# Linear attention and a SiLU MLP on one core: another token layout, two load queues, and transposes by DMA

## The chip, the cores and the metric

The kernel runs on one core of a Trainium2 chip. The metric is the device time of one execution in microseconds (us); a profile's span is the time from the first to the last instruction of one execution. Engines are named as in the profile: PE (TensorE), DVE (VectorE), ACT (ScalarE), POOL (GpSimd) and SP (SyncE); PEld is PE's weight load.

## The reference

```python
# q, k, v: (8, 8, 576, 64) float32: batch, heads, tokens, head size
def phi(x):
    return np.where(x > 0, x, np.exp(x) - 1.0) + 1.0
q_p, k_p = (phi(q), phi(k))
kv = np.einsum('bhsd,bhse->bhde', k_p, v)
z = np.sum(k_p, axis=2)
num = np.einsum('bhsd,bhde->bhse', q_p, kv)
den = np.einsum('bhsd,bhd->bhs', q_p, z)[..., None] + 1e-06
x = (num / den)            # then (batch * tokens, heads * 64) = (4608, 512)
h = x @ w_in               # w_in (512, 2048)
g = h * (1.0 / (1.0 + np.exp(-beta * h)))
out = g @ w_out            # w_out (2048, 512), out (4608, 512) float32
```

## The kernel before

The MLP runs nine times: once for each of the eight batches with its first 512 tokens, and once for the tail, the 64 last tokens of all batches together (`xT_tail`). Each run has an H phase (`h_phase`, L266: 16 groups of four products of 512 columns, and a SiLU on ACT for each group, `g`, L275) and a Y phase (`y_phase`, L291: four output tiles `y_ps` of 16 products each, a copy `y_sb` on DVE, a store by SP). So there are 18 phases of 64 products. The factor 1/beta of the SiLU form is folded into `w_out` by `w_out_scale` (L325, DVE).

Attention of a batch (`elu`, L166, and `attention`, L181) is split into steps which the phases call between their groups (`step(fill)`); nothing reorders them, so each engine takes its instructions in the order in which the code writes them. Attention 0 stands ahead of H0. Attention 1 starts inside Y0 and ends ahead of H1; attention 2, and phi of batch 3, stand in Y1; from batch 3 on attention n stands in H of batch n-1, and phi of batch n in Y of batch n-2.

Tokens of a batch lie as four per partition for the first 512 (`NJ = 4`, tiles of 128 partitions) and a fifth tile of 64 rows. phi is an exponential on ACT (L152), a maximum with 0 (L153), a minimum with 1 (L155) and an addition (L156) on DVE, each over 2560 elements per partition. `kvp` (L191) sums 4 x 5 products of 128 rows and 130 columns (64 of v and a column of ones, for two heads); DVE multiplies them with a mask that leaves the two heads' blocks (`kv_bd`). The numerator needs q with the head size on partitions, and H needs x so: both are transposed by PE against an identity (`qtp` L209, `xtp` L241, four products a token tile) into PSUM and copied by DVE (`q_pT` L213, `xT` L249). A numerator `nps` (L220, four products) gives the numerators and, in each head's 65th column, the denominators; DVE makes `den`, `rden` and `xs` (L228 to L231) of it.

Loads are all issued by POOL (`load_rows`, L62, two DMAs each, cast from fp32 to bf16 on the way), in the order k, v, q of batch 0, four pieces of `w_in`, four of `w_out` (as fp32, into buffers that are free at that time) with q, k, v of batch 1 between them. SP issues the stores and one small load. PSUM has four banks for H and Y (`mmps`), two for one numerator tile (`numps`, one buffer) and two for all else (`miscps`).

## Time and profile before

| | |
|---|---|
| Time, median of 3 runs (lowest to highest) | 358.24 us (358.24 to 358.39) |
| Span of the profiled execution | 355.9 us |
| PE busy | 307.2 us, 86%, 1793 products |
| DVE busy | 167.0 us, 47% |
| ACT busy | 153.2 us, 43% |
| POOL busy | 47.8 us, 13% |
| Bytes moved by DMA | 30.19 MB in 46133 packets |

The profile's page gives no time of the profiled execution other than its span; the median of the runs stands 2.3 us above that span. Busy times of engines overlap, so they don't add up to the span, and PE's busy time contains the latencies of products that overlap their neighbours. A stage table (busy time of each engine between two times), the chain of waits and the timeline show where PE stands still. The column PEclk is the granted clock of PE as a share of 2.4 GHz.

### The profile page before, as it was taken

The numbers are of one execution on the slowest core, as the hardware profiler recorded it, in microseconds if no ns is written. First come the engines' busy times: TensorE is split into PE (matmuls) and PEld (weight loads), VectorE is DVE, ScalarE is ACT, GpSimd is POOL, SyncE is SP. The second block draws the span as 40 slices with busy tenths as digits, with TensorE's granted clock in tenths as the row PEclk, the third lists the DMA queues.
The fourth block names the chain that finished last, engine by engine and source line by source line (L and its number), as shares of the span: only waits on it lengthen the run. The fifth ranks groups of instructions, "written<-read, shape, count | busy, mean of one in ns | idle before, by whom it ended". The sixth has DMA issues, their size and how long they took to land.

```text
span 355.9 us, 4500 instructions
## 1 busy us (share of the span) xinstructions
PE 307.2 (86%) x1793; PEld 153.5 (43%) x1793; DVE 167.0 (47%) x341; ACT 153.2 (43%) x174; POOL 47.8 (13%) x64
## 2 busy tenths in 40 slices
...
GB/s 104 192 275 252 289 175 214 219 52 57 1 168 174 110 1 2 78 207 33 2 66 118 2 0 25 96 1 2 29 90 0 2 71 47 2 59 59 0 61 60
DMA packets 46133, 30.19 MB, mean 85 GB/s; under 512 B 13840, under 2 KB 40480, under 8 KB 46112
## 3 DMA queue, kind: packets, MB, share of 16 engines
q0 software_dynamic: 40832, 20.45, 41.0%
...
HBM read 36.71 MB, written 9.44 MB: 130 GB/s over the span
## 4 chain that ended last, share of the span: by engine, by line
PE 65%; DVE 20%; issue 5%; DMA 4%; ACT 3%; POOL 1%; ACTq 0%; DVEq 0%; POOLq 0%
PE h_ps L271 30%; PE y_ps L296 25%; DVE xs L231 8%; PE xtp L241 5%; PE nps L220 3%; DMA xqk<-in_q_dram 3%; DVE rden L229 2%; ACT e L152 2%; DVE e L155 2%; DVE den L228 2%; DVE y_sb L303 2%; DMA out_dram<-y_sb 2%; PE kvp L191 1%; DVE qk_p L156 1%; DVE xT L249 1%
## 5 line engine op out<-in xcount | busy, mean ns | idle before, releaser
L275 ACT ACTIVATE g<-h_ps,beta_c 128x512 bf16<-128x512 f32 x144 | 98.5, 687 | 120.6 <-PE h_ps L271 119.9
L271 PE MATMUL h_ps<-xT,w_in 128*128 128x512 bf16 x512 | 128.6, 392 | 0.0
L296 PE MATMUL y_ps<-w_out,g 128*128 128x512 bf16 x576 | 127.3, 379 | 0.0
L296 PEld LDWEIGHTS <-g 128*128 128x128 bf16 x576 | 56.0, 98 | 65.8
L271 PEld LDWEIGHTS <-w_in 128*128 128x128 bf16 x576 | 54.1, 100 | 55.3 <-issue 6.2
L303 DVE COPY y_sb<-y_ps 128x512 f32<-128x512 f32 x36 | 24.6, 687 | 83.7 <-PE y_ps L296 77.6
L152 ACT ACTIVATE e<-xqk 128x2560 bf16<-128x2560 bf16 x16 | 36.7, 2331 | 4.6 <-DMA xqk<-in_q_dram 3.1
L241 PE MATMUL xtp<-identity,xs 128*128 128x128 bf16 (+1 forms) x160 | 17.0, 237 | 20.9 <-DVE xs L231 18.8
L155 DVE TENSOR_SCALAR e<-e 128x2560 bf16<-128x2560 bf16 x16 | 13.4, 835 | 38.0 <-ACT e L152 38.0
L275 ACT ACT_TABLE_LOAD x7 | 9.0, 1283 | 51.1 <-PE h_ps L271 51.1
L231 DVE TENSOR_TENSOR xs<-nps,rden 128x512 bf16<-128x512 f32 (+1 forms) x40 | 27.6, 689 | 1.4
L156 DVE TENSOR_TENSOR qk_p<-r,e 128x2560 bf16<-128x2560 bf16 x16 | 23.9, 1492 | 0.5
L241 PEld LDWEIGHTS <-xs 128*128 128x128 bf16 (+1 forms) x160 | 9.7, 105 | 31.3 <-DVE xs L231 31.3
L209 PE MATMUL qtp<-identity,qk_p 128*128 128x128 bf16 (+1 forms) x160 | 15.8, 227 | 6.8 <-DVE kv_bd L197 5.0
L191 PE MATMUL kvp<-vaug,qk_p 128*128 128x130 bf16 x160 | 13.1, 238 | 8.2 <-DVE qk_p L156 8.2
L209 PEld LDWEIGHTS <-qk_p 128*128 128x128 bf16 (+1 forms) x160 | 11.9, 104 | 16.3 <-issue 7.6
L213 DVE COPY q_pT<-qtp 128x512 bf16<-128x512 bf16 (+1 forms) x40 | 15.7, 395 | 6.6 <-PE qtp L209 6.3
L220 PE MATMUL nps<-kv_bd,q_pT 128*128 128x130 bf16 (+1 forms) x160 | 18.3, 244 | 0.3 <-DVE q_pT L213 0.2
...
L249 DVE COPY xT<-xtp 128x512 bf16<-128x512 bf16 x32 | 13.6, 424 | 9.3 <-PE xtp L241 8.2
L220 PEld LDWEIGHTS <-q_pT 128*128 128x128 bf16 (+1 forms) x160 | 13.2, 112 | 8.8 <-issue 2.7
L191 PEld LDWEIGHTS <-qk_p 128*128 128x128 bf16 x160 | 11.6, 107 | 12.0 <-DVE qk_p L156 8.8
...
## 6 DMA issues: line engine op xcount, KB each, us to landing
out_dram<-y_sb SPq DMA_DIRECT2D x32, 256.0 KB, 2.3
...
```

Of the source, the lines that this page charges most:

```text
L152: nc.scalar.activation(e, x, ACTF.Exp)
L155: nc.vector.tensor_scalar(e, e, 1.0, None, ALU.min)
L156: nc.vector.tensor_add(st[b, "p"][:, a].rearrange("p j (h d) -> p h j d", h=H), r, e)
L191: nc.tensor.matmul(kvp[:, pp, :], qk_p[:, 1, j, p * P : (p + 1) * P], va[:, j, 2 * p : 2 * p + 2, 0 : D + 1], start=(j == 0), stop=(j == N ...
L209: nc.tensor.matmul(tp[:, p, :n], qk_p[:n, 0, t, p * P : (p + 1) * P], identity[:n, :n], is_transpose=True, start=True, stop=True, skip_gro ...
L220: nc.tensor.matmul(nps[:n, p // 2, o : o + 2 * (D + 1)], q_pT[:, p, t * P : t * P + n], kv_bd[:, p, :], start=True, stop=True, skip_group_ ...
L231: nc.vector.tensor_mul(xs[t][:n], nv[:, :, :, 0:D], rden[:n, :, :, None].to_broadcast([n, 2, 4, D]),)
L241: nc.tensor.matmul(tp[:, p, :n], xv[:n, p * P : (p + 1) * P], identity[:n, :n], is_transpose=True, start=True, stop=True, skip_group_check ...
L271: nc.tensor.matmul(hp, w_in_sb[ff // 4][:, kc, (ff % 4) * P : (ff % 4 + 1) * P], x[:, kc, :], start=(kc == 0), stop=(kc == KC - 1),)
L275: nc.scalar.activation(g[:, ff, :], hp, ACTF.Silu, scale=beta_c[:, ff : ff + 1])
L296: nc.tensor.matmul(yp, g[:, ff, t * P : (t + 1) * P], w_out_sb[ff // 4][:, ff % 4, :], start=(ff == 0), stop=(ff == FC - 1),)
L303: nc.vector.tensor_copy(y_sb, yp)
```

## The change

All 576 tokens of a batch lie as nine per partition on 64 partitions (`G = 64`, `J = 9`); heads 0 to 3 take the lower 64 partitions and heads 4 to 7 the upper. There are no unused rows any more, and no memory clears. A token tile of a numerator takes two of the nine (four tiles of 128 columns and one of 64); the ninth tokens of all batches form the tail run. kv products have 64 rows each, 36 a batch, and change between the halves and between two PSUM tiles from one to the next (`kv_products`).

phi is min(exp(x), max(x, 0) + 1): an exponential, one DVE instruction for maximum and addition, and one minimum, each over 1152 elements, twice for k and twice for q. v is loaded as fp32 by SP and cast by POOL (for batch 0 it is cast on the way and copied by DVE). k and q are loaded by POOL with the cast; half the heads of k and q of batch 0 come by SP as fp32. `w_out` comes by SP after the third piece of `w_in`; two of its four pieces are scaled by DVE, two by POOL.

`idle` puts products of a constant tile on PE during the opening, whose results nobody reads. H0 starts with four groups of half the columns. Y0 keeps its four tiles open in four PSUM banks and does three quarters of each of them ahead of attention 1. From batch 3 on, q and x are transposed by DMAs that SP issues (`q_trans_dma`, two a batch, `x_trans_dma`, five a batch) instead of by PE; for batches 0 to 2 PE transposes and ACT (batches 0 and 1) or DVE copies. Each Y tile is stored by two DMAs of 64 partitions, from three buffers instead of two. The last Y tile is done in two pieces, of 320 and of 192 columns.

```diff
-    NJ = 4
-    MAIN = NJ * P
-    TAIL = S - MAIN
-    NT = NJ + 1
-    EA = D + 2
+    G = 64
+    J = S // G
+    NT = 5
+    EA = D + 1
...
+    xk = [consts.tile([P, 4, J, D], BF16, name=f"xk{i}") for i in range(NX)]
+    xq = [consts.tile([P, 4, J, D], BF16, name=f"xq{i}") for i in range(NX)]
+    vf = [consts.tile([P, 4, J, D], F32, name=f"vf{i}") for i in range(2)]
+    vaug = [consts.tile([P, 2, J, 2, 66], BF16, name=f"vaug{i}") for i in range(2)]
...
+    w_out_f = [
+        a.rearrange("p (c m) -> p c m", c=4)
+        for a in (g_f[:, 0:2048], g_f[:, 2048:4096], stage[:, 0:2048], stage[:, 2048:4096])
...
+    k0f = stage[:, 0:1152].rearrange("p (h j d) -> p h j d", h=2, j=J)
+    q0f = stage[:, 1152:2304].rearrange("p (h j d) -> p h j d", h=2, j=J)
...
+    def heads(src, b, hh, h0, n):
+        return src[b, hh * 4 + h0 : hh * 4 + h0 + n].rearrange(
+            "h (g j) d -> g h (j d)", j=J
...
+    def load(eng, dst, src, b, h0=0, n=4):
+        return [
+            eng.dma_start(
+                out=dst[hh * G : (hh + 1) * G].rearrange("p h j d -> p h (j d)"),
+                in_=heads(src, b, hh, h0, n),
+            )
+            for hh in range(2)
+        ]
...
+    nc.vector.memset(warm, 0.5)
+    load(nc.gpsimd, xk[0][:, 0:2], k, 0, 0, 2)
+    load(nc.sync, k0f, k, 0, 2, 2)
+    load(nc.gpsimd, xq[0][:, 0:2], q, 0, 0, 2)
+    load(nc.sync, q0f, q, 0, 2, 2)
+    beta_row = consts.tile([FC, P], F32)
+    nc.sync.dma_start(out=beta_row, in_=moe_beta.rearrange("(c p) -> c p", p=P))
+    load(nc.gpsimd, v0b[:, 0:2], v, 0, 0, 2)
+    load(nc.gpsimd, v0b[:, 2:4], v, 0, 2, 2)
...
+    load(nc.gpsimd, xk[1], k, 1)
+    load(nc.gpsimd, xq[1], q, 1)
+
+    def load_w_out(i, after=None):
+        d = nc.sync.dma_start(out=w_out_f[i], in_=w_out_v[:, i * 4 : (i + 1) * 4, :])
+        if after is not None:
+            tc.add_manual_dep(d.ins, after.ins.name, SYNC, reason="share of the queues")
...
+    def phi_part(b, a, pr, x):
+
+        e = work.tile([P, 2, J, D], BF16, tag="e", name="e", bufs=3)
+        nc.scalar.activation(e, x, ACTF.Exp)
+        st[b, a, pr, "e"] = e
+
+    def phi_relu(b, a, pr, x):
+        r = work.tile([P, 2, J, D], BF16, tag="r", name="r", bufs=3)
+        nc.vector.tensor_scalar(r, x, 0.0, 1.0, ALU.max, ALU.add)
+        st[b, a, pr, "r"] = r
+
+    def phi_tile(b, a):
+        st[b, a] = work.tile([P, 2, J, P], BF16, tag=f"phi{a}", name=f"phi_{a}")
+
+    def phi_min(b, a, pr):
+        nc.vector.tensor_tensor(
+            st[b, a][:, pr].rearrange("p j (h d) -> p j h d", h=2),
+            st[b, a, pr, "e"].rearrange("p h j d -> p j h d"),
+            st[b, a, pr, "r"].rearrange("p h j d -> p j h d"),
+            ALU.min,
...
+    def kv_products(b, prs, ps):
+        for pr in prs:
+            for j in range(J):
+                for hh in range(2):
+                    r = slice(hh * G, (hh + 1) * G)
+                    nc.tensor.matmul(
+                        ps[hh, pr],
+                        st[b, "k"][r, pr, j, :],
+                        vaug[b % 2][r, pr, j, :, 0:EA],
+                        start=(j == 0), stop=(j == J - 1), skip_group_check=True,
+                    )
...
+    def kv_both(b):
+
+        t = [miscps.tile([P, 2, 2 * EA], F32, tag="misc", name="kvp") for _ in range(2)]
+        kv_products(b, (0, 1), {(hh, pr): t[hh][:, pr] for hh in range(2) for pr in range(2)})
+        kv_tile(b)
+        for hh in range(2):
+            nc.vector.tensor_mul(
+                st[b, "kv"][:, hh], t[hh], kvmask.rearrange("p a g e -> p a (g e)")
+            )
...
+    def q_trans_dma(b):
+        st[b, "qTd"] = work.tile([P, 2, 2 * J, G], BF16, tag="qT", name="qTd")
+        for hh in range(2):
+            nc.sync.dma_start_transpose(
+                out=st[b, "qTd"][:, hh],
+                in_=st[b, "q"][hh * G : (hh + 1) * G].rearrange("p a j c -> p (a j c)"),
+            )
...
+    def x_trans_dma(b, t):
+        n = P if t < NT - 1 else G
+        nc.sync.dma_start_transpose(
+            out=x_dst(b, t),
+            in_=st[b, "xs", t][:n].rearrange("p a h d -> p (a h d)"),
+        )
...
+    def rows(b, j):
+        return out[b * S : (b + 1) * S, :].rearrange("(g j) m -> j g m", j=J)[j]
+
+    def y_out(b, t, yp, c0=0, c1=512, eng=None):
+        y_sb = work.tile([P, DM], F32, tag="y_sb", name="y_sb", bufs=3)
+        (eng or nc.vector).tensor_copy(y_sb[:, c0:c1], yp[:, c0:c1])
+        for i in range(2):
+            dst = rows(b, 2 * t + i) if b < B else rows(2 * t + i, J - 1)
+            nc.sync.dma_start(out=dst[:, c0:c1], in_=y_sb[i * G : (i + 1) * G, c0:c1])
...
+    def load_kq(b):
+        if b < B:
+            load(nc.gpsimd, xk[b % NX], k, b)
+            load(nc.gpsimd, xq[b % NX], q, b)
+
+    def load_v(b):
+        if b < B:
+            load(nc.sync, vf[b % 2], v, b)
...
+    idle(10)
...
+    phi_all(0, "k")
+    idle(6)
+    phi_all(0, "q")
+    for t in range(2):
+        q_trans(0, t, nc.vector)
+    kvp0 = {}
+    for pr in range(2):
+        v_copy(nc.vector, 0, pr)
+    kv_tile(0)
+    idle(4)
...
+    numer(0, 0)
+    numer(0, 1)
+    x_trans(0, 0, nc.scalar)
+    numer(0, 2)
+    x_trans(0, 1, nc.scalar)
...
+    for ff in range(4):
+        hps[ff] = mm_tile("h_ps")
+        h_mm(0, xT[0], ff, hps[ff], 0, 256)
+        if ff == 0:
+            numer(0, 3)
...
+    load_w_out(0, w_in_dma[2])
+    load_w_out(1)
+    load_w_out(2)
+    load_v(1)
+    load_w_out(3)
...
+    load_kq(2)
+    w_out_scale(nc.vector, 0)
+    w_out_scale(nc.vector, 1)
...
+    yps = [mm_tile("y_ps") for _ in range(4)]
+    phi_all(1, "k")
+    phi_all(1, "q")
+    for i in range(3):
+        if i == 2:
+            w_out_scale(nc.gpsimd, 2)
+        for t in range(4):
+            y_mm(0, t, i, yps[t])
+    for pr in range(2):
+        v_copy(nc.gpsimd, 1, pr)
+    w_out_scale(nc.gpsimd, 3)
+    load_v(2)
+    for t in range(3):
+        q_trans(1, t, nc.scalar)
+    kv_both(1)
+    for t in range(3, NT):
+        q_trans(1, t, nc.scalar)
+    numer(1, 0)
+    y_mm(0, 0, 3, yps[0])
+    numer(1, 1)
+    x_trans(1, 0, nc.scalar)
+    y_mm(0, 1, 3, yps[1])
...
+    for t in range(4):
+        y_out(0, t, yps[t])
+    x_trans(1, 4, nc.scalar)
...
+            if last and t == 3:
+                for c0, c1 in ((0, 320), (320, 512)):
+                    for i in range(4):
+                        y_mm(b, t, i, yp, c0, c1)
+                    y_out(b, t, yp, c0, c1)
+                break
...
+    at(sy, 11, lambda: numer(2, 2), lambda: phi_all(3, "q"))
...
+    at(sy, 14, lambda: numer(2, 4), lambda: phi_all(3, "k"))
...
-        att = lazy(attention, b + 1) if b + 1 < B else wait(0)
-        h_phase(b, xT[b % 3] if b < B else xT_tail, [att])
-        load_next(b + 3)
-        e = lazy(elu, b + 2) if b + 2 < B else wait(0)
-        y_phase(b, [att, e])
-        drain(att)
-        drain(e)
+        n = b + 1
+        sh, sy = {}, {}
+        if b == 2:
+            at(sh, 0, lambda: q_trans_dma(3), lambda: load_kq(4))
+        if n < B:
+            if n == 3:
+                at(sh, 1, lambda: [v_copy(nc.gpsimd, 3, pr) for pr in range(2)], lambda: load_v(4))
+            at(sh, 3, lambda: kv_both(n))
+            for t in range(NT):
+                at(sh, 5 + 2 * t, lambda t=t: numer(n, t))
+                at(sh, 6 + 2 * t, lambda t=t: x_trans_dma(n, t))
+        if n + 1 < B:
+            m = n + 1
+            at(sy, 0, lambda: phi_all(m, "q"))
+            at(sy, 2, lambda: q_trans_dma(m), lambda: load_kq(m + 1))
+            at(sy, 6, lambda: phi_all(m, "k"), lambda: [v_copy(nc.gpsimd, m, pr) for pr in range(2)])
+            at(sy, 7, lambda: load_v(m + 1))
+        h_phase(b, xT[b % 3] if b < B else xT_tail, sh)
+        y_phase(b, sy, last=(b == B))
```

How instructions stand now, at three places. First DVE in the steady part, from the Y copies of a batch (`y_sb`) to the first numerator of the next H phase; `kvp` and `qtp`, `xtp` are PSUM tiles. Before:

```order
L303 COPY y_sb<-y_ps 128x512 x3
L197 TENSOR_TENSOR kv_bd<-kvp,kvmask 128x260 x2
L213 COPY q_pT<-qtp 128x4x128 x2
L228 TENSOR_SCALAR den<-nps 128x8
L229 RECIPROCAL rden<-den 128x8
L231 TENSOR_TENSOR xs<-nps,rden 128x512
L213 COPY q_pT<-qtp 128x4x128
L249 COPY xT_88<-xtp 128x4x128
```

After:

```order
L141 TENSOR_SCALAR r<-xk_73 128x1152 x2
L148 TENSOR_TENSOR phi_k<-e,r 128x1152 x2
L309 COPY y_sb<-y_ps 128x512 x3
L190 TENSOR_TENSOR kv_bd<-kvp,kvmask 128x260 x2
L242 TENSOR_SCALAR den<-nps 128x8
L243 RECIPROCAL rden<-den 128x8
L245 TENSOR_TENSOR xs<-nps,rden 128x512
```

The copies of transposes are gone from between the numerators, and with them PE's products `qtp` and `xtp`.

Second, SP's queue. Before, this is all of it:

```order
L388 UNCONDITIONAL_BRANCH
L118 DMA beta_row<-in_moe_beta_dram 16x128
L283 DMA out_dram<-y_sb 128x512 x32
L287 DMA out_dram<-y_sb 64x512 x8
L388 UNCONDITIONAL_BRANCH
```

After, one steady batch from the first x transpose in an H phase on (`xs` is read, `xT` and `qTd` are written in SBUF):

```order
L271 DMA_TRANSPOSE xT_91<-xs 128x4x128 x4
L271 DMA_TRANSPOSE xT_tail<-xs 128x4x64
L217 DMA_TRANSPOSE qTd<-phi_q 128x18x64 x2
L312 DMA out_dram<-y_sb 64x512 x4
L82 DMA vf_78<-in_v_dram 64x4x576 x2
```

SP now issues the transposes and the loads of v in one queue with the stores, and the first stores of a Y phase stand behind the q transposes.

Third, DVE inside Y1, where attention 2 and phi of batch 3 stand. Before:

```order
L228 TENSOR_SCALAR den<-nps 128x8
L229 RECIPROCAL rden<-den 128x8
L231 TENSOR_TENSOR xs<-nps,rden 128x512
L155 TENSOR_SCALAR e<-e 128x2560
L156 TENSOR_TENSOR qk_p<-r,e 128x8x5x64
L153 TENSOR_SCALAR r<-xqk_72 128x2560
L303 COPY y_sb<-y_ps 128x512
L213 COPY q_pT<-qtp 128x4x128
L249 COPY xT_89<-xtp 128x4x128
```

After:

```order
L309 COPY y_sb<-y_ps 128x512
L242 TENSOR_SCALAR den<-nps 128x8
L243 RECIPROCAL rden<-den 128x8
L245 TENSOR_TENSOR xs<-nps,rden 128x512
L141 TENSOR_SCALAR r<-xq_75 128x1152 x2
L148 TENSOR_TENSOR phi_q<-e,r 128x1152 x2
L267 COPY xT_92<-xtp 128x4x128
L212 COPY qT<-qtp 128x4x64
```

phi of batch 3 still stands between the numerators of batch 2, as two pairs of smaller instructions, and it now takes q first.

## Rows read from the trace of the kernel before

**Rows 1.** Stages of the program, windows view: us, busy time per engine, clock, DMA.
```profile
core 0: us, PE busy (x) PEld busy (x) DVE busy (x) ACT busy (x) POOL busy (x), PEclk, DMA share, GB/s
0.00:32.06 32.06, 10.07 (x81) 7.85 (x82) 20.14 (x49) 7.24 (x4) 17.74 (x28) 1.00 1.18 204
32.06:47.60 15.54, 15.54 (x66) 6.72 (x65) 7.53 (x18) 10.28 (x15) 5.68 (x7) 1.00 1.32 249
47.60:75.17 27.57, 21.58 (x146) 12.08 (x144) 18.88 (x37) 7.84 (x6) 7.55 (x10) 0.84 1.38 189
75.17:91.34 16.17, 16.17 (x67) 6.89 (x65) 1.76 (x3) 10.28 (x15) 1.56 (x2) 0.85 0.33 37
91.34:120.97 29.63, 20.36 (x145) 10.86 (x144) 23.19 (x42) 11.23 (x7) 8.60 (x10) 0.94 1.00 136
120.97:295.05 174.08, 168.11 (x1043) 84.10 (x1042) 89.25 (x183) 84.33 (x97) 6.69 (x8) 0.99 0.20 43
295.05:350.47 55.42, 55.41 (x257) 24.94 (x255) 5.53 (x8) 21.98 (x32) 0.00 (x0) 1.00 0.13 38
76.00:80.00 4.00, 4.00 (x11) 1.52 (x10) 1.03 (x2) 1.37 (x2) 1.56 (x2) 0.51 0.24 24
```

**Rows 2.** Chain of waits, Y3 to Y4: start, us, engine, what.
```profile
178.59 13.81 PE y_ps L296 x64
192.41 0.86 PE h_ps L271 x4
193.27 0.58 PE kvp L191 x10
...
198.59 0.18 DVE den L228
198.79 0.21 DVE rden L229
199.03 0.70 DVE xs L231
...
212.86 1.29 PE y_ps L296 x6
```

**Rows 3.** Timeline, PE and weight loads: start, us, operation, idle before.
```profile
14.77 2.35 PE L191 MATMUL kvp<-vaug,qk_p 128*128 128x130 bf16 x20 [7.46 <-DVE qk_p L156]
...
61.42 1.31 PE L191 MATMUL kvp<-vaug,qk_p 128*128 128x130 bf16 x20
...
135.13 0.17 PEld L209 LDWEIGHTS <-qk_p 64*128 64x128 bf16 x4 [0.42 <-issue]
135.14 0.29 PE L209 MATMUL qtp<-identity,qk_p 64*128 64x64 bf16 x4
```

**Rows 4.** Groups by line and form: busy us, mean ns | idle before.
```profile
L303 DVE COPY y_sb<-y_ps 128x512 f32<-128x512 f32 x36 | 24.6, 687 | 83.7 <-PE y_ps L296 77.6 <-DMA out_dram<-y_sb 6.1
...
L152 ACT ACTIVATE e<-xqk 128x2560 bf16<-128x2560 bf16 x16 | 36.7, 2331 | 4.6 <-DMA xqk<-in_q_dram 3.1 <-DVE qk_p L156 1.5
...
L156 DVE TENSOR_TENSOR qk_p<-r,e 128x2560 bf16<-128x2560 bf16 x16 | 23.9, 1492 | 0.5
...
L153 DVE TENSOR_SCALAR r<-xqk 128x2560 bf16<-128x2560 bf16 x16 | 14.0, 878 | 0.0
...
L213 DVE COPY q_pT<-qtp 128x512 bf16<-128x512 bf16 x32 | 13.4, 422 | 6.6 <-PE qtp L209 6.3
```

**Rows 5.** DMA view: GB/s in 40 slices of 10 to 40 us; median us to landing.
```profile
GB/s 171 185 190 195 175 204 209 208 204 210 205 206 203 214 199 205 209 212 344 404 437 393 388 393 388 243 198 198 196 175 198 197 192 282 393 393 388 415 404 421
...
out_dram<-y_sb SPq DMA_DIRECT2D x32, 256.0 KB, 2.3
```

**Rows 6.** Timeline of the opening, three engines.
```profile
7.02 0.29 PE L131 MATMUL bps<-ident,beta_row 16*128 16x16 f32 x1 [7.02 <-POOL ident masks.py:199]
...
14.50 2.34 ACT L152 ACTIVATE e<-xqk 128x2560 bf16<-128x2560 bf16 x1 [3.07 <-DMA xqk<-in_q_dram]
...
17.27 0.91 POOL L63 DMA_DIRECT2D xqk<-in_k_dram  x1 [1.21 <-DMA w_in<-in_moe_w_in_dram]
```

434 lines of the change are left out of this document (201 added, 233 removed).

## The prediction, made before the result was known

> **What bounds the kernel now.** I read the stage table first [rows 1], with the stages cut where the first H or Y product of a batch starts. The eight batches and the tail batch need 18 phases of 64 products of 512 columns; an undisturbed phase takes 13.81 us [rows 2], as four pure phases show together (55.42) [rows 1]. Eighteen of them are 248.6 of the 355.9 us. The other 107 us are the subject: 32.1 before the first product, 13.8 + 15.8 in the two Y phases that carry attention 1 and 2, 4.1 lost in H0 and H1, 36 in the five H phases that carry attention 3 to 7 (174.08 - 10 x 13.81), and 5.4 after the last product. The chain of one steady batch comes next [rows 2]: H4 lasts 20.45 us, from 192.41 to 212.86. Its 80 small products (kvp, qtp, nps, xtp) cost about 0.057 us each (ten kvp: 0.58), 4.5 us together; the remaining 2.1 us are the places where PE stands until DVE has written xs and the x transposes can begin: the chain goes through den, rden and xs there. So TensorE is the bound in the steady part, and what lies between the batches' dependent steps is the bound before 121 us. ACT and DVE have slack in the steady part.
>
> **The steady part (batches 2 to 6).** The change takes q transposes, x transposes and their PSUM copies off PE and DVE (40 of the 80 small products) and gives them to SP as seven DMA transposes per batch. The kv products grow from 20 to 36, since a batch is now nine pieces of 64 rows in two partition halves; numerators stay at 20. For a 64-row product the nearest row is the q tail's transpose, four with 64 columns in 0.29 us [rows 3]: at 64 columns per 0.027 us (2.4 GHz) the four make 0.11 and 0.18 is left for the latency of the last, so they go at the column rate, as 128-row ones do. I therefore take 0.057 for each kv product of 130 columns: 36 x 0.057 = 2.05. Bounds: 1.0 if the two halves run side by side, 4 if every change of half empties the array. The weight loads of that tail wait for the products ahead (0.42 idle), while 128-row ones are loaded ahead; it costs about 0.1, and I add 0.2 for two changes. H becomes 13.81 + 2.05 + 0.2 + 20 x 0.057 = 17.2, with no xs wait, since the consumer of xs is now a DMA. A numerator comes every two groups of products (1.96 us), and den, rden and xs take 0.18 + 0.21 + 0.70 and some hops [rows 2], about 1.5, so the one PSUM tile for numerators is free in time. Y is 13.81 with 0.1 of hops; a pair is 31.1, five are **155.5** instead of 174.1. Bounds 150.5 (kv at 1.0) to 166 (kv at 4, some waits).
>
> In the trace the two-step transposes hide under nothing, so what replaces them must be hidden: the x transposes of batch n are issued in the H phase before and have at least one Y phase (13.8) until H needs them. The q transposes (b from 4) are issued some 5 us into Y and needed 6 groups into H: 15 us later. No row of before has a DMA transpose. The nearest: a 256 KB store takes 2.3 us from issue to landing, over 100 GB/s [rows 5]. Per pair the transposes move 4 x 128 + 64 + 2 x 288 KB, 1.15 MB; over 31.1 us they stay hidden if they do 37 GB/s together. I take them as hidden. Queued behind them on SP: stores of Y and loads of v; SP reaches the first stores of a Y phase only after the q transposes, which wait for phi (about 5.5 us into Y); the first Y tile is ready at 3.5, has three buffers, so nobody waits. If the cover is gone, each us over 31 costs five.
>
> By the Trainium skill, DMA: Bandwidth & Descriptors, section "Latency and other measured facts", a DMA transpose moves 261 GB/s with a non-contiguous middle dimension: an estimate by that page is 1.1 us for 288 KB, well hidden; no run here shows it yet.
>
> **The opening.** Before: q of batch 0 lands shortly before 14.50, when ACT's second exponential begins after a wait of 3.07 us for it [rows 6]; H0 starts at 32.06. In the new order k and q come first, half of each by SP, so ACT is no longer last. DVE is: ident16 now stands behind eight DMA issues of POOL instead of six (0.7 to 0.91 us each [rows 6]), so the beta product goes from 7.02 [rows 6] to about 8.4, and DVE takes beta (1.1) ahead of the first relu: 9.6. Phi in quarters: relu of 1152 elements 0.45 (0.88 for 2560 [rows 4]; 0.65 from fp32), minimum 0.72 (1.49 for 2560), so 2 x (0.45 + 0.65 + 1.44) = 5.1 and hops: phi q at 15, where before its exponential had only begun. Copies of q transposes and v, 1.6, kv 36 products at 0.057, or at 0.107 at the lower clock: 2 to 3.9. (20 kvp took 2.35 us at 14.77, 1.31 at 61.42 [rows 3]: the first at the pace of the lower level, 1.2 GHz, though the clock column shows 1.00 for the opening.) Then two numerators with their x transposes, about 1.65 a piece, and H0 starts its first half-width groups at about 25.5; the other halves wait for the fifth x tile, 29.4. H0 ends 13.81 - 1.73 later (four half-width groups are 1.73): **41.5** (before 47.60). Bounds 40 to 46. Loads don't speed up: one queue reads w_out at 390 to 420 GB/s already [rows 5] (the rows at half of it are loads cast to 2 bytes). First need of w_in is later than its landing (17.3 before [rows 6], about 1.4 later now), w_out waits for the third w_in piece, about 24, and after that 11 MB on both queues take 28 us: the last w_out is there at about 52, and POOL's four scalings (no row has one; 0.5 to 1 us each taken) end at 55. Y0 needs it at 57.
>
> The Trainium skill speaks against this part: DMA: Bandwidth & Descriptors, "Rules for kernel authors", says that transfers spread over several issuing engines, or to disjoint partition halves, share the same engines and gain no bandwidth. The rate of one queue here agrees; by that rule only the order of the loads can gain, which is all that I count.
>
> **Y0 with attention 1.** Three quarters of all four Y0 tiles go first: 10.36 us, under which ACT (table 1.28, four exponentials of 1.05 from 2.33 for 2560 [rows 4]) and DVE make phi. Then q transposes with ACT copies (0.69 taken, as DVE's Y copy of as many elements [rows 4]), 2.5; kv 2.3; masks and the last transposes 1.4; five numerators through one PSUM tile, 0.25 + 1.1 + hops 0.3 each, 8.2, with the last quarters of Y0 beside them; a Y copy that frees the first H bank, 0.7. Sum 10.4 + 15.2 = **25.6** (before 27.57). Bounds 24 to 29. H1 pays 16.17 before: the clock was granted at 0.51, its lower level of 1.2 GHz, through 76 to 80 [rows 1], after a stage with little PE work. With Y quarters in between the stage is fuller; I take **14.4** (13.8 to 16.2).
>
> **Y1 with attention 2 and phi 3.** DVE's list here: phi 2 and 3, 4 x 2.34 = 9.4; five numerators 5.7; q and x copies 4.0 (0.42 each, 0.29 the tails [rows 4]); masks 0.85; four Y copies 2.75: 22.7, and it begins 3.2 after the stage's start (table, first exponential); PE and DVE wait for each other about 1 us more. **27.0** against 29.63 (DVE 23.19 busy there [rows 1]). Bounds 26 to 30. v copies go to POOL, out of the way.
>
> **The end.** Four pure phases 55.4 as before. The last tile is cut at 320 columns, so the last copy is 0.3 instead of 0.69: 5.0 instead of the 5.43 that lie between 350.47 and 355.9.
>
> **Sum.** 41.5 + 25.6 + 14.4 + 27.0 + 155.5 + 55.4 + 5.0 = 324.4 of span. The page gives no time beside the span; the median of three runs, 358.24, is 2.3 above 355.9, and I add the same: **326.7**, 31.5 under before. By terms: steady 18.6, opening 6.1, Y0 2.0, H1 1.8, Y1 2.6, end 0.4.
>
> **Rivals.**
> (a) The halves of the kv products run side by side: 1.0 instead of 2.05 in five steady batches, as much in attention 1, about 2 in attention 0: 8 us less, **318.7**. For it: nothing in the trace alternates halves; the four 64-row ones share one half. Beside it the Trainium skill, TensorE: Matmul & The Clock Gate, "Part 3: Packing small matmuls — row/col tiling", says that products on different row groups run concurrently. The trace neither shows nor denies it.
> (b) Transposes take the place of the waits. At 36 GB/s, 8 us for 288 KB: in H2 the first numerator needs two of them 8 us after SP can issue them (behind the last Y1 store, while k and q of batch 4 load), so 8 late, and 32 per pair in place of 31.1: **340**.
> (c) Slower than before: the same mechanism below 31 GB/s. A pair then needs (358.2 - 326.7)/5 = 6.3 us more than 31.1, 37.4 us for 1.15 MB; at 25 GB/s it is 46 us and the time **401**. Against it: stores at over 100 GB/s. [...]
> (d) The opening does not do what it says: with two queues at 300 GB/s in sum the last w_out comes at 61, not 52, Y0 waits 6: **333**.
>
> **Chances.** Forecast 0.5, (a) 0.2, (b) 0.13, (c) 0.08, (d) 0.09. Range 314 to 345: from the forecast with its terms at their lower bounds and (a) up to (b) with some opening loss; (c) and the far side are left out. Faster by over 0.2% 0.91, same (0.2%, about what a measurement of this kernel can tell) 0.01, slower 0.08.
>
> **What would show it.** Right: H phases of batches 2 to 6 near 17.2, with no PE wait on xs and none on qTd; Y at 13.8; H0 starting near 25.5; Y1 to H2 bounded by DVE. (a): 36 kv products in about 1 us. (b), (c): numerators waiting on DMA qTd, or h_ps on xT. (d): POOL or DVE scaling waiting for w_out. The forecast is wrong if one transpose lands more than some 5 us after its issue, or if kv takes over 3 us.

## The result, and the profile after

The changed kernel takes **328.81 us** (median of four runs, 326.5 to 329.88) against 358.24 in the same comparison: a ratio of 0.917, 95% interval 0.911 to 0.924. The profiled execution took 329.76 us, its span is 328.0. Forecast were 326.7 and a span of 324.4.

The windows view of the changed kernel, cut at the same places as [rows 1] (the cut at 28.73 is the first H0 product; the line at 47.35 begins with Y0, whose first product is at 47.19; 70.5 H1, 90.79 Y1, 114.61 H2, 267.88 the four pure phases, 323.95 the end). Columns as in [rows 1]: start:end, us, busy time of each engine, granted clock, DMA share, GB/s.

```profile
0.00:28.73 28.73, 15.08 (x95) 7.55 (x96) 13.39 (x36) 8.24 (x10) 13.86 (x28) 0.72 1.08 207
28.73:47.35 18.62, 17.56 (x100) 9.98 (x101) 6.16 (x17) 12.54 (x19) 3.27 (x3) 0.89 1.11 280
47.35:70.50 23.15, 19.75 (x157) 10.36 (x156) 11.77 (x25) 11.38 (x16) 19.56 (x18) 1.00 0.75 150
70.50:90.79 20.29, 16.92 (x63) 7.02 (x66) 2.59 (x5) 11.60 (x17) 2.23 (x2) 0.83 0.80 168
90.79:114.61 23.82, 18.98 (x157) 10.42 (x157) 18.96 (x45) 11.90 (x11) 2.60 (x4) 1.00 0.45 83
114.61:267.88 153.27, 152.27 (x905) 73.41 (x921) 60.10 (x137) 82.53 (x104) 14.05 (x16) 0.99 0.65 120
267.88:323.95 56.07, 55.19 (x267) 26.18 (x270) 6.03 (x10) 21.98 (x32) 0.00 (x0) 1.00 0.18 40
323.95:328.00 4.05, 0.00 (x0) 0.00 (x0) 0.36 (x1) 0.00 (x0) 0.00 (x0) 0.81 0.21 48
```

Beside the forecast's terms:

| stage | before, us | forecast | after | missed by |
|---|---|---|---|---|
| up to the end of H0 | 47.60 | 41.5 | 47.35 | +5.85 |
| Y0 with attention 1 | 27.57 | 25.6 | 23.15 | -2.45 |
| H1 | 16.17 | 14.4 | 20.29 | +5.89 |
| Y1 with attention 2 and phi 3 | 29.63 | 27.0 | 23.82 | -3.18 |
| five steady pairs | 174.08 | 155.5 | 153.27 | -2.23 |
| four pure phases | 55.42 | 55.4 | 56.07 | +0.67 |
| end | 5.43 | 5.0 | 4.05 | -0.95 |
| span | 355.9 | 324.4 | 328.0 | +3.6 |

That the sum came within 3.6 us is luck in good part: two terms are too low by nearly 6 us each, and 8.8 us of terms that are too high hide most of that. The opening gained next to nothing (47.35 against 47.60), and H1 became 4 us slower than before. The experiments go after these two first, then after the steady part.

The longest pieces of the chain of waits up to H1 (start, us, what), in the changed kernel, name both places:

```profile
3.51 8.03 DMA beta_row<-in_moe_beta_dram
...
71.08 6.31 DMA out_dram<-y_sb
78.25 11.89 PE h_ps L279 x41
```

The first: beta, 8 KB, is issued by SP at 3.51 us, behind four fp32 loads of k and q, and lands 8.03 us later. (POOL's four loads of k and q were issued ahead of it too, on the other queue, and the last of them landed just before it, at 11.39.) The timeline of DVE (start, us, operation, idle before and its releaser) shows what stood behind it: five small operations on beta, and only then the first relu, whose input was there by 8.80, when ACT, which waits for the same load, begins.

```profile
11.97 0.17 DVE L348 COPY beta_s<-bps 128x16 f32<-128x16 f32 x1 [9.56 <-PE bps L343]
...
12.98 0.40 DVE L141 TENSOR_SCALAR r<-xk 128x1152 bf16<-128x1152 bf16 x1
```

The second: Y0's four tiles now end together, there are three y_sb buffers, and the fourth copy waits for a store. The waits view of DVE (who, for whom: us in total, times, longest):

```profile
DVE y_sb L309 <- DMA out_dram<-y_sb: 5.8, 1, 5.8
```

And the timeline of PE behind it:

```profile
70.52 4.49 PE L279 MATMUL h_ps<-xT,w_in 128*128 128x512 bf16 x19 [0.31 <-DVE y_sb L309]
78.25 12.54 PE L279 MATMUL h_ps<-xT,w_in 128*128 128x512 bf16 x43 [3.24 <-DVE y_sb L309]
```

PE makes five groups of H1, then stands 3.24 us until DVE has made the fourth copy. The granted clock was 1.00 from 71 to 77 and 0.52 from 77 to 84: it fell to the lower level (1.2 GHz) during that stand, so H1 pays twice.

### The profile page after: what moved, and what is told of

The parts are those of the page before. It is cut to its first block, busy times and chain, and to the rows that moved or that the text cites. A ratio compares the mean times of both kernels' runs of the same rounds, so it can differ in the third digit from the quotient of the medians.

```text
span 328.0 us, 4511 instructions
## 1 busy us (share of the span) xinstructions
PE 295.7 (90%) x1739; PEld 144.9 (44%) x1767; DVE 119.4 (36%) x272; ACT 160.2 (49%) x208; POOL 55.6 (17%) x70
## 4 chain that ended last, share of the span: by engine, by line
PE 82%; DVE 7%; DMA 4%; issue 3%; ACT 2%; SPq 1%; DVEq 0%
PE h_ps L279 38%; PE y_ps L297 36%; PE nps L234 4%; PE kvp L174 3%; DMA beta_row<-in_moe_beta_dram 2%; DVE xs L245 2%; DMA out_dram<-y_sb 2%; DVE y_sb L309 1%; PE qtp L202 1%; SPq L82 1%; DVE rden L243 1%; ACT qT L210 1%; DVE r L141 1%; DVE phi_q L148 1%; PE xtp L260 1%
## 5 line engine op out<-in xcount | busy, mean ns | idle before, releaser
L279 PE MATMUL h_ps<-xT,w_in 128*128 128x512 bf16 (+1 forms) x513 | 122.8, 386 | 8.5 <-DVE y_sb L309 3.5
L297 PE MATMUL y_ps<-w_out,g 128*128 128x512 bf16 (+2 forms) x580 | 127.2, 374 | 1.3 <-DVE y_sb L309 0.6
L309 DVE COPY y_sb<-y_ps 128x512 f32<-128x512 f32 (+2 forms) x37 | 24.8, 673 | 88.0 <-PE y_ps L297 82.2
L164 POOL CAST vaug<-vf 128x1152 bf16<-128x1152 f32 x14 | 16.6, 1214 | 123.2 <-DMA vf<-in_v_dram 98.1
L148 DVE TENSOR_TENSOR phi_k<-e,r 128x1152 bf16<-128x1152 bf16 x16 | 12.1, 787 | 25.6 <-ACT e L136 25.6
L136 ACT ACTIVATE e<-xk 128x1152 bf16<-128x1152 bf16 x15 | 16.7, 1151 | 7.5 <-DVE phi_q L148 7.4
L148 DVE TENSOR_TENSOR phi_q<-e,r 128x1152 bf16<-128x1152 bf16 x16 | 11.8, 753 | 13.9 <-ACT e L136 13.9
L136 ACT ACTIVATE e<-xq 128x1152 bf16<-128x1152 bf16 x15 | 16.5, 1151 | 0.0
L317 POOL TENSOR_SCALAR w_out<-stage,rbeta 128x512 bf16<-128x512 f32 x8 | 12.6, 1591 | 20.8 <-DMA stage<-in_moe_w_out_dram 20.8
L279 PE MATMUL h_ps<-xT_tail,w_in 128*128 128x512 bf16 x63 | 13.9, 379 | 0.1
```

Source lines behind the costliest of these rows:

```text
L136: nc.scalar.activation(e, x, ACTF.Exp)
L148: nc.vector.tensor_tensor(st[b, a][:, pr].rearrange("p j (h d) -> p j h d", h=2), st[b, a, pr, "e"].rearrange("p h j d -> p j h d"), st[b, ...
L164: eng.tensor_copy(vaug[b % 2][:, pr, :, :, 0:D], src[:, 2 * pr : 2 * pr + 2].rearrange("p h j d -> p j h d"),)
L279: nc.tensor.matmul(hp[:, c0:c1], w_in_sb[ff // 4][:, kc, (ff % 4) * P : (ff % 4 + 1) * P], x[:, kc, c0:c1], start=(kc == 0), stop=(kc == K ...
L297: nc.tensor.matmul(yp[:, c0:c1], g_sb[b % 2][:, ff, t * P : (t + 1) * P], w_out_sb[i][:, c, c0:c1], start=(ff == 0), stop=(ff == FC - 1), ...
L309: (eng or nc.vector).tensor_copy(y_sb[:, c0:c1], yp[:, c0:c1])
```

## Experiments

All times are medians; the kernel before took 356.9 to 358.2 us beside them. Each kernel is the changed kernel with the edit shown, unless said otherwise. The changed kernel itself was not run again beside them, and its own four runs lie 3.4 us apart: a difference of one or two us from 328.81 is read from the stages of the two profiles, not from the medians.

### Beta first on SP

```diff
+    beta_row = consts.tile([FC, P], F32)
+    nc.sync.dma_start(out=beta_row, in_=moe_beta.rearrange("(c p) -> c p", p=P))
     load(nc.gpsimd, xk[0][:, 0:2], k, 0, 0, 2)
     load(nc.sync, k0f, k, 0, 2, 2)
...
-    beta_row = consts.tile([FC, P], F32)
-    nc.sync.dma_start(out=beta_row, in_=moe_beta.rearrange("(c p) -> c p", p=P))
```

> The 8 KB load of beta goes first on SP, ahead of the four fp32 loads of k and q. Theory A (the opening was missed because beta landed at 11.5 us behind those loads and DVE has beta ahead of the first relu): beta lands by about 5, the beta product goes when ident16 is ready (about 7), the first relu starts when xk is there, about 9 to 9.5 instead of 12.98, and everything up to the first H0 product comes 3.0 to 3.5 us earlier; the time falls from 328.8 to about 325.5. Rival B (the loads or the low granted clock between 20 and 34 us set the opening): the first relu is earlier, but the first H0 product moves by less than 1 us, and the time stays within 1 us of 328.8.

Measured: 325.91 us (325.27 to 327.57), ratio to before 0.913 (0.909 to 0.916), 2.9 less than the changed kernel. Timeline of DVE and PE in this run:

```profile
7.40 0.17 DVE L348 COPY beta_s<-bps 128x16 f32<-128x16 f32 x1 [4.98 <-PE bps L343]
...
8.41 0.47 DVE L141 TENSOR_SCALAR r<-xk 128x1152 bf16<-128x1152 bf16 x1
...
24.15 0.86 PE L279 MATMUL h_ps<-xT,w_in 128*128 128x256 bf16 x4 [0.67 <-ACT xT L265]
...
51.49 2.97 PE L297 MATMUL y_ps<-w_out,g 128*128 128x512 bf16 x13 [1.44 <-POOL w_out L317]
...
60.82 0.38 PE L297 MATMUL y_ps<-w_out,g 128*128 128x512 bf16 x1 [1.17 <-POOL w_out L317]
```

The first relu comes at 8.41 instead of 12.98, H0 at 24.15 instead of 28.73, Y0 at 42.33 instead of 47.19 (A; the forecast had 41.5). Part of these 4.9 us is the clock, which differs from execution to execution: in the four later profiles with beta first and the same dummy products Y0 begins at 42.43 to 44.20. So the load's place in SP's queue cost 3.0 to 4.9 us, most of the opening's loss. 2.5 us are given back in Y0 (25.80 instead of 23.33), where PE now waits 1.44 and 1.17 us for POOL's scaling of w_out: in the changed kernel that scaling, 1.59 us each, was hidden only because the opening was late.

### Four y_sb buffers

```diff
-        y_sb = work.tile([P, DM], F32, tag="y_sb", name="y_sb", bufs=3)
+        y_sb = work.tile([P, DM], F32, tag="y_sb", name="y_sb", bufs=4)
...
-    warm = consts.tile([P, 512], BF16, name="warm")
+    warm = g_sb[0][:, 0, :]
```

> Four y_sb buffers instead of three (room is made by giving the dummy products a part of g0 as operand). Theory A (H1 lasts 20.29 us because Y0's fourth copy waits 5.85 us for a store that competes with loads of k and q, and the granted clock falls afterwards): the fourth copy follows the third at about 71.7, H1 takes 14 to 15.5 us, the time is about 323.5. Rival B (the clock falls anyway after the thin stage with attention 1, as it did in the kernel before, where H1 took 16.17): H1 about 17, time about 325.5. Rival C (the next wait, four later stores that land just as late, takes its place): no change.

Measured: 323.62 us (321.51 to 323.93), ratio 0.904 (0.900 to 0.908), 5.2 less than the changed kernel. H1 in the windows view of this run, columns as above:

```profile
71.07:84.89 13.82, 13.82 (x65) 6.28 (x65) 2.47 (x5) 11.56 (x17) 0.00 (x0) 1.00 0.94 215
```

H1 is a pure phase, at a granted clock of 1.00 (A, and 0.6 us better than the forecast's 14.4). So the low clock of H1 in the changed kernel was no consequence of the stage before it, as rival B had it: here, where PE isn't made to stand in H1, it doesn't fall.

### Three buffers, but no loads beside the stores

```diff
 def load_kq(b):
-            load(nc.gpsimd, xk[b % NX], k, b)
-            load(nc.gpsimd, xq[b % NX], q, b)
+            ds = load(nc.gpsimd, xk[b % NX], k, b)
+            ds += load(nc.gpsimd, xq[b % NX], q, b)
+            if b == 3:
+                for d in ds:
+                    tc.add_manual_dep(d.ins, st["y0"].ins.name, SYNC, reason="share of the queues")
...
-        (eng or nc.vector).tensor_copy(y_sb[:, c0:c1], yp[:, c0:c1])
+        cp = (eng or nc.vector).tensor_copy(y_sb[:, c0:c1], yp[:, c0:c1])
+        if (b, t) == (0, 3):
+            st["y0"] = cp
```

> Three y_sb buffers as in the changed kernel, but the loads of k and q of batch 3 (and batch 4's, which stand behind them on POOL) wait for Y0's fourth copy. Theory A (the store that the fourth copy waits for takes 6.3 us because it shares the DMA engines with 4.7 MB of such loads): the stores land in 2.4 to 3.5 us, the fourth copy waits 2 to 3 us instead of 5.85, time about 325. Rival B (the stores are slow by themselves, or by v's load on the same queue): 5.85 us of wait again, time 328.8.

Measured: 324.80 us (323.82 to 325.51), ratio 0.909 (0.904 to 0.913). The DMA issues between 60 and 82 us (KB each, median us from issue to landing) in the changed kernel:

```profile
xk<-in_k_dram POOLq DMA_DIRECT2D x4, 288.0 KB, 6.2
xq<-in_q_dram POOLq DMA_DIRECT2D x4, 288.0 KB, 8.7
...
out_dram<-y_sb SPq DMA_DIRECT2D x8, 128.0 KB, 6.3
```

The same view between 60 and 85 us in this run:

```profile
out_dram<-y_sb SPq DMA_DIRECT2D x8, 128.0 KB, 2.4
```

And DVE's timeline in it:

```profile
73.59 0.69 DVE L309 COPY y_sb<-y_ps 128x512 f32<-128x512 f32 x1 [1.91 <-DMA out_dram<-y_sb]
```

Without the loads the same stores land in 2.4 instead of 6.3 us (A). The 1.91 us of wait that are left don't reach PE: its H1 is 13.82 us here too (Y1, though, is 25.84 us instead of 23.98: the load of batch 3's v now runs beside those of k and q, and POOL's cast of it, from 89.09 on, falls beside DVE's phi; see the last section). In the changed kernel POOL, done with the scalings at 62.03, had run ahead and issued the loads of batches 3 and 4, of which the first is needed in Y1 and the second in Y2; nothing in the code holds them back.

### kv products by halves

```diff
             for j in range(J):
-                for hh in range(2):
+            for hh in range(2):
+                for j in range(J):
```

(inside the loop over `pr`, the rest of the body unchanged)

> The same 36 kv products per batch, but nine of one partition half and then nine of the other, instead of alternating. Theory A (36 take 1.16 us because two products on different partition halves run side by side): they take about 2.05 us (36 x 0.057), so 0.9 us more in each of batches 1 to 7, 6 us in all, some of it hidden in attention 1 and 2: time 333 to 335. Rival B (a 64-row product simply takes half as long, 0.032 us, whatever stands next to it): 1.16 us again, time 328.8.

Measured: 329.88 us (327.56 to 331.84), ratio 0.921 (0.916 to 0.926). The timeline of PE for the kv products of one steady batch, the changed kernel first, then this one:

```profile
150.13 1.23 PE L174 MATMUL kvp<-vaug,phi_k 64*128 64x130 bf16 x36
```
```profile
150.57 1.63 PE L174 MATMUL kvp<-vaug,phi_k 64*128 64x130 bf16 x36
```

Neither number that was expected. The nanoseconds between the starts of the products in that batch, from the trace, tell why:

```
alternating: 4 65 3 57 4 53 3 57 3 54 3 57 3 53 ...
by halves:   67 62 56 60 57 8 52 17 40 21 39 18 62 56 9 51 16 41 ...
```

Alternating, the products start in pairs 3 or 4 ns apart, and the next pair follows 53 to 57 ns later: each product takes its full time, and two on different halves run together. In blocks, products of one half follow each other at 56 to 67 ns, and around a change of half the other half's products start between them (the trace doesn't name the halves; this is read from the spacing). So B is refuted (a 64-row product alone costs 56 to 67 ns, not 32), and A holds, with the addition that some products near a change overlap even in blocks. The order is worth 0.4 us per batch (a steady pair takes 30.69 us here, 30.28 alternating); the 1.1 us between the medians are within the spread of the runs.

### PE and DVE transposes in the steady part too

```diff
-            at(sh, 0, lambda: q_trans_dma(3), lambda: load_kq(4))
+            at(sh, 0, lambda: load_kq(4))
...
+                at(sh, 4 + 2 * t, lambda t=t: q_trans(n, t, nc.vector))
                 at(sh, 5 + 2 * t, lambda t=t: numer(n, t))
-                at(sh, 6 + 2 * t, lambda t=t: x_trans_dma(n, t))
+                at(sh, 7 + 2 * t, lambda t=t: x_trans(n, t, nc.vector))
...
-            at(sy, 2, lambda: q_trans_dma(m), lambda: load_kq(m + 1))
+            at(sy, 2, lambda: load_kq(m + 1))
```

> Batches 3 to 7 are transposed by PE with copies by DVE, as batches 1 and 2 are, instead of by DMA; spread over the groups of the H phase. Theory A (the DMA transposes hide completely, and the steady gain is the 40 small products and the waits that left PE): each H phase gets 40 x 0.057 = 2.3 us, and 0 to 2 us of waits, so 11.5 to 21 us in all: time 340 to 350. Rival B (the steady gain came from the layout and the spread, waits included, and the products themselves are cheap): less than 8 us more, under 337.

Measured: 340.82 us (338.24 to 341.01), ratio 0.952 (0.947 to 0.956), 12.0 more than the changed kernel, at the lower end of A's range. The timeline of PE in this run: a pair, from kv products to kv products, with one transpose of each kind.

```profile
152.32 1.22 PE L174 MATMUL kvp<-vaug,phi_k 64*128 64x130 bf16 x36
...
156.53 0.39 PE L202 MATMUL qtp<-identity,phi_q 128*128 128x128 bf16 x4
...
157.62 0.39 PE L260 MATMUL xtp<-identity,xs 128*128 128x128 bf16 x4
...
184.82 0.35 PE L174 MATMUL kvp<-vaug,phi_k 64*128 64x130 bf16 x6
```

A pair is 32.50 us here, 30.28 with DMA transposes (150.13 to 180.41), 34.27 before ([rows 2], 178.59 to 212.86). The 40 small products are 2.2 us of a pair, 0.055 each, and they are all that the DMA transposes save: PE shows no wait for a releaser in these five pairs. The other 1.8 us are not the DMA's; they came with the rest of the change (spreading the steps of a batch over the groups, which leaves PE no wait, and the layout), and no run parts these.

### Both mends, and what stood behind them

> Beta first on SP and four y_sb buffers together. In their own runs they gave 2.9 and 5.2 us. Theory A (two independent losses, one ahead of Y0, one in H1): they add, 328.8 - 8.1 = 320.7. Rival B (both end in the same wait: with beta first, Y0 was already seen to wait 2.6 us for POOL's w_out scaling, and an earlier H1 meets the loads earlier): 322 to 323.6.

Beta first and four buffers together: 322.04 us (320.94 to 323.36), ratio 0.901 (0.896 to 0.906), B's number. B's reason is not shown: POOL's scaling is the wait in Y0 again, but with 0.65 us on `w_out`, not 2.6. What A's sum lacks stands in this profile in the opening, at a lower clock than in the run with beta first alone (H0 at 25.74 instead of 24.15), and in Y1 (24.96 instead of 24.00).

The next kernel puts the loads of batch 2's k and q behind POOL's scalings and gives DVE half of the scalings of w_out's third and fourth piece:

```diff
-    load_kq(2)
     w_out_scale(nc.vector, 0)
     w_out_scale(nc.vector, 1)
...
-            w_out_scale(nc.gpsimd, 2)
+            w_out_scale(nc.gpsimd, 2, 2)
+            w_out_scale(nc.vector, 2, 0, 2)
...
-    w_out_scale(nc.gpsimd, 3)
+    w_out_scale(nc.gpsimd, 3, 2)
+    w_out_scale(nc.vector, 3, 0, 2)
+    load_kq(2)
```

> On top of beta first and four y_sb buffers: the loads of k and q of batch 2 go behind POOL's scalings instead of ahead of them, and DVE takes half of the scalings of the last two w_out pieces. Theory A (what is left in Y0 is POOL, 1.6 to 1.8 us per scaling, and the last w_out piece, which lands at 54.5 because batch 2's k and q share the DMA engines with it): the waits of 1.44 and 1.17 us in Y0 go, 2.4 us less than beta first with four buffers, 318 to 319. Rival B (w_out's own loads bind, at the rate of the DMA engines): the last piece lands as late and the time stays at that of the run with the two changes alone.

Measured: 322.12 us (321.5 to 323.68), ratio 0.902 (0.897 to 0.907): no gain, but not for B's reason. POOL's and DVE's timelines in this run, and PE's:

```profile
40.22 3.11 POOL L317 TENSOR_SCALAR w_out<-stage,rbeta 128x512 bf16<-128x512 f32 x2 [24.89 <-DMA stage<-in_moe_w_out_dram]
...
51.25 2.62 DVE L317 TENSOR_SCALAR w_out<-stage,rbeta 128x512 bf16<-128x512 f32 x4
...
52.21 3.79 PE L297 MATMUL y_ps<-w_out,g 128*128 128x512 bf16 x16 [2.69 <-DVE w_out L317]
```

The third piece of w_out is there at 40.22, where POOL began at 44.56 in the run before this, and the last at 49.07 instead of 54.37: the loads that were moved had held them up. But I had put DVE's half behind phi 1, so PE waited for DVE instead of POOL.

The next kernel scales that half before phi 1, and in Y1 puts relu and minimum of phi 3 behind the copies of the x transposes, for which PE had waited 1.70 and 2.71 us:

```diff
     w_out_scale(nc.vector, 1)
+    w_out_scale(nc.vector, 2, 0, 2)
...
             w_out_scale(nc.gpsimd, 2, 2)
-            w_out_scale(nc.vector, 2, 0, 2)
...
-    at(sy, 11, lambda: numer(2, 2), lambda: phi_all(3, "q"))
+    at(sy, 11, lambda: numer(2, 2), lambda: phi_exp(3, "q"))
...
-    at(sy, 13, lambda: numer(2, 3), lambda: x_trans(2, 2, nc.vector))
-    at(sy, 14, lambda: numer(2, 4), lambda: phi_all(3, "k"))
-    at(sy, 15, lambda: x_trans(2, 3, nc.vector), lambda: x_trans(2, 4, nc.vector))
+    at(sy, 13, lambda: numer(2, 3), lambda: x_trans(2, 2, nc.vector), lambda: phi_rest(3, "q"))
+    at(sy, 14, lambda: numer(2, 4), lambda: phi_exp(3, "k"))
+    at(sy, 15, lambda: x_trans(2, 3, nc.vector), lambda: x_trans(2, 4, nc.vector), lambda: phi_rest(3, "k"))
```

(`phi_exp` makes the exponentials, `phi_rest` relu and minimum)

> From the version with beta first, four y_sb buffers and the k and q loads of batch 2 behind POOL's scalings. Two orders on DVE are changed: its half of w_out's third piece is scaled before phi 1 instead of behind it (PE waited 2.69 us for it in Y0), and the second half of phi 3 (relu and minimum) comes behind the copies of the x transposes that Y1 and H2 need (PE waited 1.70 us in Y1 and 2.71 us at the start of H2 for those copies). Theory A (DVE's order is what is left in these three places): the three waits go, 5 to 7 us less than 322.1, 315 to 317. Rival B (what stands behind DVE, the last w_out load, the exponentials and the lower clock, comes up within a microsecond): 319 to 321.

Measured: 319.66 us (318.45 to 320.2, five runs), ratio 0.895 (0.892 to 0.897). Less than A, and B's range. In the profile the wait in Y0 is gone, and Y0 is 23.34 us instead of 26.37 (44.17 to 67.51; the version before, 42.44 to 68.81). At the start of H2 PE waits 0.64 instead of 2.71. What took part of it back stands ahead of Y0: H0 begins at 25.71 instead of 24.26, in a stretch that these edits don't touch (the first of them acts at 40.85). The pace of PE differs there: the same 36 kv products of batch 0 take 2.13 us instead of 1.23, at a granted clock of 0.58 instead of 0.76 between 14 and 21 us.

### The clock of the opening

> The 20 dummy products of the opening are left out. Theory A (they hold the granted clock up for the kv products, the numerators and the first half-width groups): the clock is at its lower level longer between 16 and 34 us, the opening takes 1.5 to 4 us more, 330 to 333. Rival B (the granted clock was at its lower level between 9 and 22.7 us and between 26 and 33 us with them, and what bounds the opening are DVE's chain and the loads): within 1 us of 328.8.

The changed kernel without its 20 dummy products (10 + 6 + 4, the three calls of `idle` taken out): 330.22 us (328.94 to 330.45), ratio 0.923 (0.917 to 0.929). H0 begins at 29.26 instead of 28.73 and Y0 at 46.93 instead of 47.19. The time lies in A's range, but the opening is not longer, and the two profiled spans differ by 0.3 us: A's reason is not shown, and the 1.4 us between the medians are within the spread of the runs. The changed kernel's dummies didn't hold the clock up; the windows view of its opening shows it at the lower level in two stretches:

```profile
9.00:22.70 13.70, 8.02 (x57) 4.16 (x58) 8.56 (x20) 5.51 (x5) 6.66 (x10) 0.50 1.23 205
26.00:33.00 7.00, 5.33 (x36) 3.95 (x36) 3.09 (x9) 1.76 (x3) 0.00 (x0) 0.51 1.13 286
```

(Without dummies the trace has no record of the clock before 31.5 us, and the column shows 1.00 there, as it does for the opening in [rows 1]; that is no reading. The pace is that of the lower level, 2.13 us for the 36 kv products of batch 0.)

Three kernels went together, to see what the clock does once beta no longer holds the opening: the best version again, one with more dummies, one without any.

> The version with all changes so far, beside the next two on the same chip: 318.5 to 320.2 as before. In its profile the granted clock stands at its lower level at 13 to 20 and 23 to 30 us, and H0 begins at 25.7.

318.34 us (318.24 to 318.75), ratio 0.890 (0.885 to 0.895). H0 begins at 24.26 and not at 25.7, with 1.46 us for the 36 kv products of batch 0 and the clock up from 17.7 to 24.5 us: one and the same kernel has openings that differ by 1.45 us.

```diff
     numer(0, 0)
+    idle(4)
     numer(0, 1)
     x_trans(0, 0, nc.scalar)
+    idle(3)
     numer(0, 2)
     x_trans(0, 1, nc.scalar)
+    idle(2)
```

> Nine more dummy products (four, three and two) in the three gaps of 1.2, 1.0 and 0.7 us in which PE waits for xs and xT ahead of H0. Theory A (the lower clock at 23 to 30 us comes after PE stood idle in those gaps): the clock stays up, four half-width products take 0.60 instead of 1.01 us, H0 ends 1.5 us earlier, time 1 to 2 us less. Rival B (the dummies, at the lower clock, only delay what stands behind them): the same, or up to 1 us more.

**316.64 us** (315.2 to 317.6), ratio 0.885 (0.879 to 0.891), the best of all. The windows view from 24.5 to 28 us, of the best version and of this one (the last three columns are clock, DMA share, GB/s):

```profile
24.50:28.00 3.50, 3.50 (x24) 2.55 (x21) 1.09 (x4) 0.58 (x1) 0.00 (x0) 0.51 1.14 270
```
```profile
24.50:28.00 3.50, 3.12 (x32) 2.31 (x31) 2.25 (x7) 1.17 (x2) 0.00 (x0) 1.00 1.14 267
```

And the timelines of PE, in the same order:

```profile
22.95 0.41 PE L234 MATMUL nps<-kv_bd,qT 128*128 128x130 bf16 x4 [1.00 <-DVE xs L245]
...
24.26 0.81 PE L279 MATMUL h_ps<-xT,w_in 128*128 128x256 bf16 x4 [0.67 <-ACT xT L265]
```
```profile
23.20 0.41 PE L234 MATMUL nps<-kv_bd,qT 128*128 128x130 bf16 x4 [0.35 <-DVE xs L245]
...
24.50 0.60 PE L279 MATMUL h_ps<-xT,w_in 128*128 128x256 bf16 x4 [0.24 <-ACT xT L265]
```

The nine dummies fill the gaps between dependent steps, the clock stays at its upper level, and Y0 begins at 41.28 instead of 42.43 although the first H0 group is 0.24 us later. In the best version the clock fell after those gaps, and so it did in all ten profiles with the 20 dummies and the gaps left open, somewhere between 3.0 us ahead of the first H0 group and 0.3 us behind it. Only with the gaps filled it didn't, which is A's mechanism. Not all of the size is A's: of the 1.87 us between the two profiled spans, 1.15 stand at Y0's start, and 0.75 in H2 (17.29 instead of 18.04), which the nine dummies don't touch. There the clock fell in the one profile, from 103.0 to 106.4, and stayed up in the other, behind the same wait of PE (0.64 us). In the medians the gain is 1.7 us; every run of this version is below every run of the other, but the intervals of the ratios overlap.

> The same version without any dummy product. Theory A (dummies matter once beta no longer holds the opening): the clock is at its lower level until the first long stretch of H0 products, and the time 1 to 3 us more than best2_again. Rival B (as in the run without dummies before, they change little): within 1 us.

318.48 us (318.11 to 318.69), ratio 0.890 (0.885 to 0.895), the same as best2_again (B). In the profiles two differences cancel. Its H0 begins 1.2 us later (25.46), at the lower clock (2.13 us for the 36 kv products of batch 0, half-width groups of 1.01), and Y0 1.34 us later (43.77); and its Y1 is 1.61 us shorter (22.01 instead of 23.62). The timelines of POOL and DVE in Y1, of best2_again and of this one:

```profile
83.00 3.37 POOL L164 CAST vaug<-vf 128x1152 bf16<-128x1152 f32 x2 [18.44 <-DMA vf<-in_v_dram]
85.28 1.91 DVE L141 TENSOR_SCALAR r<-xq 128x1152 bf16<-128x1152 bf16 x2
```
```profile
82.65 2.24 POOL L164 CAST vaug<-vf 128x1152 bf16<-128x1152 f32 x2 [19.39 <-DMA vf<-in_v_dram]
86.09 0.81 DVE L141 TENSOR_SCALAR r<-xq 128x1152 bf16<-128x1152 bf16 x2
```

In best2_again POOL's casts of v run beside DVE's phi of batch 2, and both take longer; here phi comes 1.36 us later and the casts are nearly over. So equal times don't show that the 20 dummies do nothing. They may be worth 1.3 us of opening, but that is less than one kernel's openings differ by, and the next collision took it back.

## Why the prediction was right, and where it was wrong

**The steady part: right, one term mis-sized.** 153.27 against 155.5. A repeating pair takes 30.28 us (forecast 31.1): H was forecast at 17.2 and is 16.5 (146.58 to 163.05), with no wait of PE for qTd, xs or xT. The first pair takes 1.9 us more. Ahead of H2 PE stands for DVE's copies of the last transposes, and the clock is at its lower level from 114.8 to 118.3:

```profile
114.61 0.82 PE L279 MATMUL h_ps<-xT,w_in 128*128 128x512 bf16 x2 [2.71 <-DVE xT L267]
```

The term that was too big is kv: 36 x 0.057 = 2.05 plus 0.2, where 1.16 was needed between the start of the first kv product and the next H product; that is **rival (a)**'s mechanism, for which the chance was put at 0.2. By the Trainium skill, TensorE: Matmul & The Clock Gate, "Part 3: Packing small matmuls — row/col tiling", products on different row groups run concurrently; the start times above agree, with 53 to 57 ns per pair. The rival's price was nearly right as well (1.0 in place of 2.05); its total was not reached for reasons that have nothing to do with kv. The numerators (0.24 each) and the Y phase are as forecast.

**The DMA transposes: hidden, as forecast, but not as fast as the medians say.** The DMA view of the changed kernel (median us from issue to landing):

```profile
qTd<-phi_q SPq DMA_TRANSPOSE x10, 4.8
xT<-xs SPq DMA_TRANSPOSE x20, 2.4
xT_tail<-xs SPq DMA_TRANSPOSE x5, 2.3
```

And the lines that issue them on SP (ns min/median/max of the issue, first and last start), each followed by the landing times of that tile's transposes:

```profile
L217 SPq DMA_TRANSPOSE qTd<-phi_q x10: 1253/1838/3455, 115.5 to 230.2; - x10
...
DMA to landing us min/median/max: 3.9/4.8/5.4
...
L271 SPq DMA_TRANSPOSE xT<-xs x20: 1188/1190/1704, 124.3 to 251.3; - x20
...
DMA to landing us min/median/max: 2.4/2.4/9.5
```

4.8 us for 288 KB (60 GB/s, and two go at once) and 2.4 us for 128 KB are, in the median, above the 37 GB/s at which the transposes would just have stayed hidden. By the Trainium skill, DMA: Bandwidth & Descriptors, "Latency and other measured facts", 288 KB at 261 GB/s would be an estimate of 1.1 us; here the transposes took over four times that, and the measurement decides. Eight of the 35 transposes took over 5 us; x transposes issued while POOL's loads of k and q ran took up to 9.5, that is 14 GB/s. By the prediction's own sign (one transpose landing more than some 5 us after its issue) it should then have failed. It didn't: PE waited for none of them in the changed kernel, since a Y phase of 13.8 us stands between an x transpose and its use. So the sign was set too tight, and it is that distance, not the speed, that hides them. The one tight place is where rival (b) put it, H2: in five of the kernels above (not in the changed one) its first numerator waited 0.5 to 2.0 us, here in the run without dummies:

```profile
123.15 0.29 PE L234 MATMUL nps<-kv_bd,qTd 128*128 128x130 bf16 x2 [1.76 <-DMA qTd<-phi_q]
```

**The opening: wrong, by 5.85 us.** Two steps failed. The first (3.2 us up to H0's start) is "ident16 now stands behind eight DMA issues of POOL instead of six [...], so the beta product goes from 7.02 [rows 6] to about 8.4". The product needs two inputs. I followed ident16 through POOL's queue and not beta_row through SP's, where the change puts four large loads ahead of it; it landed at 11.5, while ident16 was ready at 7.0. From the first relu to H0 it then took 15.75 us, about as forecast (9.6 to 25.5), though the steps listed there come to 23.8 at most and leave out the masks and a third numerator.

The second (2.5 us) is H0 itself, 16.0 us in the forecast (25.5 to 41.5) and 18.46 in the run. Its four half-width groups, with what stands between them, were taken at the upper clock: 3.9 us, and it is 3.89 where the clock stays up (24.50 to 28.39 with the gaps filled), but 5.57 where the lower level lasts to 32.9 (28.73 to 34.30). Behind them PE waits for a SiLU ahead of which ACT loads a table (1.28 us), which the forecast had in Y0 but not here:

```profile
36.83 10.52 PE L279 MATMUL h_ps<-xT,w_in 128*128 128x512 bf16 x47 [0.61 <-ACT g L287]
```

With beta first H0 begins 1.35 us ahead of the forecast and lasts 2.2 longer, so its end at 42.33 is near 41.5 by two misses of opposite sign. Rival (d) named another resource: the opening's loss was not the rate of the loads but the place of the smallest of them, and the clock. One more step was covered only by this loss: scalings taken as 0.5 to 1 us each on POOL take 1.59 (and the last piece of w_out lands at 55.5, not 52), and would have shown in Y0.

**H1: wrong, by 5.89 us.** The failed step is 14.4, a phase without a wait: 13.82 with four buffers, 20.11 with three. The forecast weighed only the clock after a thin stage, and called stores off the path ("three buffers, so nobody waits", said of the steady Y phases). Y0 over four banks makes four copies at once with three buffers; and POOL issues the loads of two further batches right behind its scalings, so beside these stores. [rows 5] shows a store of before landing in 2.3 us; that was taken as its price wherever it stands.

**Y0 and Y1: too high, by 2.45 and 3.18 us.** In Y0 the terms for q transposes (2.5) and kv (2.3) were each too long: kv took 1.21, the transposes 1.96, since they overlap with their copies on ACT, and masks with the last transposes 0.9 instead of 1.4; the numerators came as forecast, one per 1.63 us. In Y1 the structure was right: DVE begins 3.4 us into the stage (forecast 3.2) and has little idle time from there on, and PE waits 1.69 and 2.71 us for its copies. The list was too long: 22.7 in the forecast, 18.96 in the run. 0.8 of it, the relus of phi 2's k, had been done in H1 already; and I added single instructions, where two in a row overlap (two relus 0.82, two minima 1.41, where one takes 0.45 and 0.75).

**Pure phases and end: right in sum** (60.12 against 60.4). The cut of the last tile shortens the end to 4.05, but costs a wait of 0.6 us between its two parts, since the second part's products wait for the copy of the first. (The 2.3 us added to the span for the time were 1.76 in the profiled run.)
